# Retention outputs as 64x64 products, issued among the states and the scores of a chunked attention kernel

## The chip, the cores and the metric

The kernel runs on one core of one Trainium2 chip. The metric is device time in microseconds (us) of one launch; the kernel before takes 735.98 us, the median of three runs (735.45 to 736.35). A core has five engines with queues of their own: PE (matmuls, TensorE), DVE (VectorE), ACT (ScalarE), POOL (GpSimd) and SP, which here only issues DMAs; ACT can issue DMAs too.

## The reference, cut to what matters

Three layers follow one another. The change lies in the first.

```
# 1. retention: q, k, v are (8, 8, 576, 64): batch, head, position, head_dim
ret = (q @ k^T / 8) * Dmat          # Dmat = gamma_head ** (i - j) for i >= j, else 0
x   = (ret @ v)  as  (4608, 512)
# 2. x = h * sigmoid(1.702 h) @ w_out,  h = x @ w_in       (512 -> 2048 -> 512)
# 3. soft mixture of experts: logits = x @ phi, softmax over tokens -> 32 slots,
#    two dense layers per expert, softmax over slots -> combine
```

## The kernel before

**Blocks.** The 4608 tokens are 12 blocks of 384. For a block n the big product `hp` (line 316, `main_fc`) takes x(n) times 16 column pieces of w_in, each as 12 matmuls (a split of x and w in a high and a low part), ACT makes `gT` of it (L318), DVE transposes `gT` into a staging buffer (L339, `turn_fc`), and 16 small DMAs on SP's queue carry half a block from there to `nat` (L346, `shuffle`). Logits (`Lg`), the softmax (`lt`, `dp`) and slot sums (`Sg`) of the block before are fitted in between.

**Retention in steps.** x comes from 36 steps, three a block. A step takes one chunk of 64 positions for 2 batches (`NSEQ`) and all 8 heads, that is 4 pairs of heads (`NP`). Every group of 9 steps (`NPB`) goes through one sequence. For each chunk there are three kinds of product, all in fp32 and all 64 columns wide:

- scores `Sp` = K Q (L198), one 64x64 product for each head, two heads of a pair on the two halves of the partitions;
- the running state `St` += K V (L194), 64x64 too;
- the output `Op` (L221, L222): for each head one product over 128 partitions, whose upper and lower halves hold, side by side, scaled state beside raw values (the stationary operand) and raw Q beside decayed scores (the moving one). So state times Q and values times scores are summed in one pass. Its result has 64 rows, so a matmul fills a 128x64 half of the array.

To have these operands stacked, the host lays K, Q, V of the two heads of a pair on opposite halves, a step is loaded by two DMAs of 512 KB (SP lower half, ACT upper half, `load_step`, L165 and L166), and DVE writes the scaled state (L207, L208) and the decayed scores (L212, L213) back into `pack` in four instructions of 64 partitions each. For the first step of a sequence POOL writes zeros in place of the state (L210, L211). POOL scales K (L203). Then DVE scales `Op` to `xs` (L228), ACT casts it to x (L230) and POOL makes the low part (L231).

**Order.** The step of a block's window is called at fc = 4, 9 and 13 of the 16 pieces (`WINDOWS`): first `load_step`, then `step_out` (16 `Op` products), then `products` (16 `St` and 16 `Sp` for the next chunk, interleaved). From block 1 to 10 PE's order is the order of the code (`manual_schedule`); the other engines' order, and PE's in the start (the list `START`, blocks 0 and the first six steps), is set by a scheduler when the program is built. Every engine runs its own list in order. In the start w_in and w_out come in 32 pieces of 512 KB on SP's queue into seven buffers, are converted from 64 bits by ACT, DVE and POOL (L267 to L293) and six of these buffers share their memory with `nat`.

Of the kernel before, what the change touches and what calls it, by code (L numbers as in the profile page):

```python
# [18 lines left out]
B, H, S, D = 8, 8, 576, 64  # L19
# [94 lines left out]
def tile_kernel(ctx, tc, qkv, w_in, w_out, phi, w1, w2, consts, out):  # L114
    nc = tc.nc
    pe, act, dve, pool, sp = nc.tensor, nc.scalar, nc.vector, nc.gpsimd, nc.sync

    pp = ctx.enter_context(tc.tile_pool(name="pp", bufs=1))
    ps = ctx.enter_context(tc.tile_pool(name="ps", bufs=1, space=PSUM))
# [5 lines left out]
    pg = gate_ctx.enter_context(tc.tile_pool(name="pg", bufs=1, reuse_waits="tile"))  # L125
    pb = ctx.enter_context(tc.tile_pool(name="pb", bufs=1, side="right", reuse_waits="tile"))
# [27 lines left out]

    Q1, V0, KT, KN, Q0, V1 = range(6)
    early_raw = pm.tile([128, 6, 1024], F32, tag="nat", name="early_raw")
    packs = [pa.tile([128, 6, NP, NSEQ, C], F32, name=f"pack{i}", bufs=1) for i in range(NPACK)]
    pool.memset(packs[0][0:C, V0], 0.0)  # L160
    pool.memset(packs[0][C:128, V1], 0.0)

    def load_step(g):
        t = packs[g % NPACK].rearrange("p c a j d -> p (c a j d)")
        sp.dma_start(t[0:C, KT * PC:6 * PC], qkv[g, 0:C])  # L165
        act.dma_start(t[C:128, 0:Q0 * PC], qkv[g, C:128])  # L166

    how = {"sub": {}}
    St = {}
    xh, xl = {}, {}  # L170
    halves = (slice(0, C), slice(C, 128))

    def by_head(table, r):
        return table[r].unsqueeze(2).to_broadcast([C, NP, NSEQ, C])

    def by_state(table, r):
        return table.unsqueeze(2).unsqueeze(3).to_broadcast([r, NP, NSEQ, D])

    def products(g):

        n = g + 1
        more = g >= 0 and g % NPB < NPB - 1
        if more:
            if g % NPB == 0:
                St[g // NPB] = ps.tile([128, NP, NSEQ, D], F32, tag="St", name="St")
            s_, t = St[g // NPB], packs[g % NPACK]
        if n < NSTEP:
            u = packs[n % NPACK]
            Sp = ps.tile([128, NP, NSEQ, C], F32, tag="r", name="Sp", bufs=3)
        for p in range(NP):  # L190
            for j in range(NSEQ):
                if more:
                    for h, v in zip(halves, (V1, V0)):
                        pe.matmul(s_[h, p, j, :], t[h, KN, p, j], t[h, v, p, j], start=g % NPB + p + j == 0, stop=True,  # L194
                                  skip_group_check=True)
                if n < NSTEP:
                    for h, o, q in zip(halves, halves[::-1], (Q0, Q1)):
                        pe.matmul(Sp[o, p, j, :], u[h, KT, p, j], u[h, q, p, j], start=True, stop=True)  # L198
        if n == NSTEP:
            return  # L200
        cb = n % NPB
        if cb < NPB - 1:
            pool.tensor_tensor(u[:, KN], u[:, KN], by_state(ksc[:, cb, :], 128), op=ALU.mult)  # L203
        lo, hi = halves
        if more:
            sc = stsc[:, cb, :]
# [8 lines left out]
    def step_out(g):  # L215
        n, i = divmod(g, STEPS)
        t = packs[g % NPACK]
        Op = ps.tile([128, NP, NSEQ, C], F32, tag="r", name="Op", bufs=3)
        for p in range(NP):
            for j in range(NSEQ):  # L220
                pe.matmul(Op[0:C, p, j, :], t[:, V0, p, j], t[:, Q0, p, j], start=True, stop=True)  # L221
                pe.matmul(Op[C:128, p, j, :], t[:, V1, p, j], t[:, Q1, p, j], start=True, stop=True)  # L222
        if n not in xh:
            x = (pg if n % 2 == LAST % 2 else pb).tile([128, 2, NDC, NB], F32R, tag="x", name="x", bufs=1)
            xh[n], xl[n] = x[:, 0], x[:, 1]
        cols_ = slice(i * CP, (i + 1) * CP)
        xs = pa.tile([128, NP, NSEQ, C], F32, tag="xs", name="xs")
        dve.tensor_tensor(xs, Op, osc.unsqueeze(2).to_broadcast([128, NP, NSEQ, C]), op=ALU.mult)  # L228
        flat = xs.rearrange("p a j c -> p a (j c)")
        act.copy(xh[n][:, :, cols_], flat)  # L230
        pool.tensor_tensor(xl[n][:, :, cols_], flat, xh[n][:, :, cols_], op=ALU.subtract)  # L231

    def step_of(g):
        if g + NPACK - 1 < NSTEP:
            load_step(g + NPACK - 1)
        step_out(g)
        products(g)

    wt = {}
    wide = w_in.dtype != F32  # L240
# [34 lines left out]
    def make_wp(i):  # L275
        r0 = 2 * (i % 2)
        for j in range(2):
            fc = 2 * i + j
            wo, free = ring[:, r0 + j, 0], ring[:, r0 + j, 1]
            upper, lower = load_raw((w_out.bitcast(I32) if wide else w_out)[fc * 128:(fc + 1) * 128, :], None)  # L280
            if wide:
                act.activation(upper.bitcast(F32), upper.bitcast(F32), AF.Prelu, scale=2.0 ** -112, alpha=2.0 ** 32)
                dve.tensor_scalar(lower, lower, 29, None, op0=ALU.logical_shift_right)
                dve.scalar_tensor_tensor(wo.bitcast(I32), upper, 3, lower, op0=ALU.logical_shift_left,
                                         op1=ALU.bitwise_or)
            else:
# [13 lines left out]
        dve.transpose(Wp[:, 2 * i:2 * i + 2, :], wps)  # L300
# [227 lines left out]
    n = LAST  # L528
# [18 lines left out]
    n = LAST  # L547
# [203 lines left out]
```

## Time and profile before

| | |
|---|---|
| median of 3 runs | 735.98 us |
| the profiled execution | 738.28 us, span 736.5 us |
| PE busy | 675.6 us (92%) |
| DVE, ACT, POOL busy | 349.5, 230.9, 103.1 us |
| chain that ended last | PE 77%, DMA 9%, DVE 7%, SP's queue 4% |

The profiled execution lies 2.30 us over the median. PE's matmuls overlap, so a long busy time is no sum of their costs; what a matmul costs is read from the distance between the starts of two that follow each other. The span has four parts: the start up to the first `hp`, block 0, an uneven passage into block 1 and ten even blocks of some 47.4 us, then the last block and the third layer.

### The profile page before, as it was taken

What the parts mean: (1) busy time and instruction counts of PE and PEld (TensorE: products, weight loads), DVE (VectorE), ACT (ScalarE), POOL (GpSimd) and SP (SyncE); (2) the same over time, 40 slices, a digit from 0 to 9 for tenths busy, and PEclk for the clock granted to TensorE, in tenths of its full rate; (3) what the DMA queues carried; (4) which work ended last, traced back from release to release, by engine and by line L of the source; (5) the groups of instructions that cost most, each with busy time, mean ns of one, the idle gap of its engine ahead of it and who ended that gap; (6) DMA issues with size and microseconds to landing.
All of it is one profiled execution on the core that took longest, in us unless ns stands there. A gap on an engine that the chain in (4) does not pass through costs nothing.

```text
span 736.5 us, 17854 instructions
## 1 busy us (share of the span) xinstructions
PE 675.6 (92%) x7512; PEld 567.7 (77%) x7512; DVE 349.5 (47%) x964; ACT 230.9 (31%) x431; POOL 103.1 (14%) x93
## 2 busy tenths in 40 slices
PE   2549999699999999999999999999999999978995
PEld 2438879589879899897998988989879788743563
DVE  0786962533554545436454464544554523131233
ACT  0436652222412324123241241332412325231332
POOL 1234320111111111111111021111110000001000
PEclk9769999989999999999999999999999999999999
DMA  9999987638476475574864738637466069899978
GB/s 209 284 294 318 334 237 165 133 75 171 101 152 160 96 156 127 117 165 100 166 145 98 168 80 183 159 82 157 112 144 145 10 204 320 322 409 408 410 285 322
DMA packets 72527, 142.17 MB, mean 193 GB/s; under 512 B 9600, under 2 KB 51840, under 8 KB 67840
## 3 DMA queue, kind: packets, MB, share of 16 engines
q1 hardware_dynamic: 67264, 117.97, 57.1%
q10 hardware_dynamic: 5184, 23.07, 13.3%
q8 instruction: 59, 0.97, 0.6%
q14 instruction: 20, 0.16, 0.1%
HBM read 92.77 MB, written 13.63 MB: 144 GB/s over the span
## 4 chain that ended last, share of the span: by engine, by line
PE 77%; DMA 9%; DVE 7%; SPq 4%; issue 1%; ACT 1%; DVEq 0%; ACTq 0%
PE hp L316 49%; DMA early_raw<-in_moe_w_in_dram 6%; PE Sg L413 5%; PE Op L221 4%; PE Lg L353 4%; PE St L194 3%; PE h_ps L600 3%; PE so_ps L664 3%; SPq L346 2%; DMA pack<-in_qkv_dram 2%; DMA nat<-pre 2%; PE Sp L198 1%; DVE pre L339 1%; SPq L255 1%; PE op L686 1%
## 5 line engine op out<-in xcount | busy, mean ns | idle before, releaser
L316 PE MATMUL hp<-x,w 128*128 128x384 f32 x2304 | 424.1, 341 | 7.6 <-ACT x L230 7.0
L316 PEld LDWEIGHTS hp<-x,w 128*128 128x128 f32 x2304 | 401.3, 189 | 34.9 <-issue 18.6
L318 ACT ACTIVATE gT<-hp 128x384 f32<-128x384 f32 x192 | 94.1, 491 | 317.7 <-PE hp L316 317.6
L339 DVE STREAM_TRANSPOSE ring<-gT 128x128 f32<-128x128 f32 x240 | 55.9, 284 | 120.1 <-ACT gT L318 120.1
L339 DVE STREAM_TRANSPOSE pre<-gT 128x128 f32<-128x128 f32 x288 | 65.3, 281 | 87.8 <-ACT gT L318 77.0
L231 POOL TENSOR_TENSOR x<-xs,x 128x512 fp32r<-128x512 f32 x36 | 46.6, 1296 | 242.7 <-ACT x L230 236.8
L203 POOL TENSOR_TENSOR pack<-pack,cs 128x512 f32<-128x512 f32 x32 | 34.4, 1075 | 179.0 <-DMA pack<-in_qkv_dram 151.7
L198 PE MATMUL Sp<-pack 64*64 64x64 f32 x1152 | 44.2, 228 | 13.5 <-DMA pack<-in_qkv_dram 13.5
L198 PEld LDWEIGHTS Sp<-pack 64*64 64x64 f32 x1152 | 38.6, 140 | 14.5 <-DMA pack<-in_qkv_dram 13.5
L194 PE MATMUL St<-pack 64*64 64x64 f32 x1024 | 40.6, 230 | 9.3 <-DVE pack L208 8.9
L221 PEld LDWEIGHTS Op<-pack 128*64 128x64 f32 x576 | 38.4, 143 | 12.5 <-issue 7.5
L221 PE MATMUL Op<-pack 128*64 128x64 f32 x576 | 44.0, 231 | 4.4 <-DVE pack L212 4.4
L194 PEld LDWEIGHTS St<-pack 64*64 64x64 f32 x1024 | 35.4, 142 | 14.6 <-issue 12.3
L353 PE MATMUL Lg<-gT,Wp 128*32 128x384 f32 x384 | 43.8, 496 | 0.0
L222 PE MATMUL Op<-pack 128*64 128x64 f32 x576 | 43.0, 231 | 0.0
L230 ACT CAST x<-xs 128x512 fp32r<-128x512 f32 x36 | 22.2, 618 | 52.3 <-DVE xs L228 43.8
L222 PEld LDWEIGHTS Op<-pack 128*64 128x64 f32 x576 | 38.0, 143 | 0.4
L413 PE MATMUL Sg<-nat,dn 128*32 128x512 f32 x288 | 35.7, 615 | 0.3 <-DVE dn L397 0.3
L212 DVE TENSOR_TENSOR pack<-Sp,cs 64x512 f32<-64x512 f32 x36 | 25.0, 694 | 11.0 <-PE Sp L198 10.2
L228 DVE TENSOR_TENSOR xs<-Op,cs 128x512 f32<-128x512 f32 x36 | 24.5, 682 | 5.4 <-PE Op L222 5.4
L207 DVE TENSOR_TENSOR pack<-St,cs 64x512 f32<-64x512 f32 x32 | 22.2, 693 | 8.6 <-PE Sp L198 8.4
L413 PEld LDWEIGHTS Sg<-nat,dn 128*32 128x32 f32 x288 | 9.5, 113 | 20.5 <-issue 19.7
(111 smaller groups left out, 485.0 us busy)
## 6 DMA issues: line engine op xcount, KB each, us to landing
wx<-in_moe_w_dram SPq DMA_DIRECT2D x60, 512.0 KB, 10.2
pack<-in_qkv_dram ACTq DMA_DIRECT2D x36, 512.0 KB, 7.5
pack<-in_qkv_dram SPq DMA_DIRECT2D x36, 512.0 KB, 6.9
nat<-pre SPq DMA_DIRECT2D x192, 96.0 KB, 2.3
nat<-ring SPq DMA_DIRECT2D x160, 96.0 KB, 2.2
out_dram<-ob SPq DMA_DIRECT2D x16, 512.0 KB, 3.9
early_raw<-in_moe_w_in_dram SPq DMA_DIRECT2D x14, 512.0 KB, 12.3
early_raw<-in_moe_w_out_dram SPq DMA_DIRECT2D x14, 512.0 KB, 9.3
```

Of the source, the lines that this page charges most:

```text
L194: pe.matmul(s_[h, p, j, :], t[h, KN, p, j], t[h, v, p, j], start=g % NPB + p + j == 0, stop=True, skip_group_check=True)
L198: pe.matmul(Sp[o, p, j, :], u[h, KT, p, j], u[h, q, p, j], start=True, stop=True)
L203: pool.tensor_tensor(u[:, KN], u[:, KN], by_state(ksc[:, cb, :], 128), op=ALU.mult)
L212: dve.tensor_tensor(u[hi, Q0], Sp[hi], by_head(dtab, hi), op=ALU.mult)
L221: pe.matmul(Op[0:C, p, j, :], t[:, V0, p, j], t[:, Q0, p, j], start=True, stop=True)
L222: pe.matmul(Op[C:128, p, j, :], t[:, V1, p, j], t[:, Q1, p, j], start=True, stop=True)
L231: pool.tensor_tensor(xl[n][:, :, cols_], flat, xh[n][:, :, cols_], op=ALU.subtract)
L316: pe.matmul(hp, wt[fc][:, a, dc, :], b[n][:, dc, :], start=(i == 0), stop=(i == 3 * NDC - 1))
L318: act.activation(gT[n, g][:, fl, :], hp, AF.Gelu_apprx_sigmoid)
L339: dve.transpose(dst[:, c], src[:, c])
L353: pe.matmul(Lg[n][32 * fl:32 * fl + 32, :], Wp[:, g * GF + fl, :], gT[n, g][:, fl, :], start=(g == 0), stop=(g == NFC // GF - 1))
L413: pe.matmul(Sg[32 * b:32 * b + 32], dn[n][:, c, :], nv[:, 4 * b:4 * b + 4], start=(c == 0), stop=(c == NT128 - 1))
```

## The change

The output product of a head is taken apart in two 64x64 products that add up in the same place: state times Q (`SS`, `QT`), then values times decayed scores (`VN`, `SC`); at the first chunk of a sequence the first of them is left out. All planes of a head now lie on the same 64 partitions, a step is loaded by one DMA of 1 MB on SP's queue, and `pack` has planes of their own for `SC` and `SS`. DVE writes each by one instruction over 128 partitions, and POOL's zeros are gone. `window` takes the place of `step_out` and `products`: it lists the step's own products (`St`, then `Sp` of the next chunk) and its output products, and issues them in turn, a pair of the one and a pair of the other.

```diff
     def load_step(g):
-        t = packs[g % NPACK].rearrange("p c a j d -> p (c a j d)")
-        sp.dma_start(t[0:C, KT * PC:6 * PC], qkv[g, 0:C])
-        act.dma_start(t[C:128, 0:Q0 * PC], qkv[g, C:128])
+        sp.dma_start(packs[g % NPACK].rearrange("p c a j d -> p (c a j d)")[:, 0:4 * PC], qkv[g])
...
+            for p, j in pairs:
+                if cb:
+                    out_.append((Op, t, SS, QT, p, j, True))
+                out_.append((Op, t, VN, SC, p, j, cb == 0))
...
+            own += [(s_, t, KN, VN, p, j, g % NPB + p + j == 0) for p, j in pairs]
...
+            own += [(Sp, u, KT, QT, p, j, True) for p, j in pairs]
+        for i in range(max(len(own), len(out_))):
+            for what, turn in ((own, 0), (out_, 1)):
+                if i < len(what):
+                    o, w, a, b, p, j, first_ = what[i]
+                    for h, oh in ((lo, (lo, hi)[turn]), (hi, (hi, lo)[turn])):
+                        pe.matmul(o[oh, p, j, :], w[h, a, p, j], w[h, b, p, j], start=first_, stop=True,
                                   skip_group_check=True)
...
+            dve.tensor_tensor(u[:, SC], Sp, across(dtab), op=ALU.mult)
+            if more:
+                dve.tensor_tensor(u[:, SS], s_, by_state(stsc[:, n % NPB, :]), op=ALU.mult)
...
-            dve.tensor_tensor(u[lo, V0], s_[hi], by_state(sc[hi], C), op=ALU.mult)
-            dve.tensor_tensor(u[hi, V1], s_[lo], by_state(sc[lo], C), op=ALU.mult)
-        elif g >= 0:
-            pool.memset(u[lo, V0], 0.0)
-            pool.memset(u[hi, V1], 0.0)
-        dve.tensor_tensor(u[hi, Q0], Sp[hi], by_head(dtab, hi), op=ALU.mult)
-        dve.tensor_tensor(u[lo, Q1], Sp[lo], by_head(dtab, lo), op=ALU.mult)
...
-        for p in range(NP):
-            for j in range(NSEQ):
-                pe.matmul(Op[0:C, p, j, :], t[:, V0, p, j], t[:, Q0, p, j], start=True, stop=True)
-                pe.matmul(Op[C:128, p, j, :], t[:, V1, p, j], t[:, Q1, p, j], start=True, stop=True)
```

PE's order in an even block, at a window (before; the pair of `Op` rows stands eight times, the pair of `St` and `Sp` rows eight times):

```order
L316 MATMUL hp<-x,w 128x384 x84
L221 MATMUL Op<-pack_93 64x64
L222 MATMUL Op<-pack_93 64x64
...
L194 MATMUL St<-pack_93 64x64 x2
L198 MATMUL Sp<-pack_94 64x64 x2
...
L353 MATMUL Lg<-gT,Wp 32x384 x4
L316 MATMUL hp<-x,w 128x384 x12
L366 MATMUL lt<-Lp,sum4r 128x384 x2
```

The same kind of place in the changed kernel (each pair of rows eight times):

```order
L305 MATMUL hp<-x,w 128x384 x24
L202 MATMUL St<-pack_94 64x64 x2
L202 MATMUL Op<-pack_94 64x64 x2
...
L202 MATMUL Sp<-pack_95 64x64 x2
L202 MATMUL Op<-pack_94 64x64 x2
...
L342 MATMUL Lg<-gT,Wp 32x384 x8
```

A window has 64 matmuls in place of 48, and `Op` ends with the window and no longer at its middle.

SP's order at the end of the start, from the last pieces of w_out to block 0's two sets of `nat` transfers (before):

```order
L255 DMA early_raw<-in_moe_w_out_dram 128x1024 x3
L165 DMA pack_94<-in_qkv_dram 64x2048
L455 DMA wx<-wo_dram 128x1024
L346 DMA nat<-pre 32x3x256 x16
L165 DMA pack_95<-in_qkv_dram 64x2048
L455 DMA ring<-in_moe_w_dram 128x1024
L346 DMA nat<-pre 32x3x256 x16
```

And in the changed kernel:

```order
L244 DMA early_raw<-in_moe_w_out_dram 128x1024 x4
L444 DMA wx<-wo_dram 128x1024
L162 DMA pack_94<-in_qkv_dram 128x2048
L335 DMA nat<-pre 32x3x256 x16
L162 DMA pack_95<-in_qkv_dram 128x2048
L335 DMA nat<-pre 32x3x256 x16
L444 DMA ring<-in_moe_w_dram 128x1024
```

The load into `pack_94` stands as a whole ahead of the first `nat` transfers; before, SP issued its lower half one row earlier, and ACT its upper half from its own list. The prefetch into `ring` moves behind the second `nat` transfers.

## Rows read from the trace of the kernel before

**Rows 1.** The page: busy time, then the chain that ended last.

```profile
PE 675.6 (92%) x7512; PEld 567.7 (77%) x7512; DVE 349.5 (47%) x964; ACT 230.9 (31%) x431; POOL 103.1 (14%) x93
...
PE 77%; DMA 9%; DVE 7%; SPq 4%; issue 1%; ACT 1%; DVEq 0%; ACTq 0%
```

**Rows 2.** Busy us of each engine in three stretches, granted clock, DMA share, GB/s.

```profile
13.00:54.08 41.08, 19.92 (x352) 18.01 (x352) 28.65 (x46) 14.07 (x22) 12.26 (x9) 0.75 1.06 282
54.08:107.20 53.12, 51.81 (x635) 43.71 (x635) 41.09 (x84) 31.11 (x56) 18.79 (x14) 0.97 0.98 305
...
146.87:597.30 450.43, 447.67 (x5024) 393.42 (x5024) 225.76 (x679) 127.52 (x233) 62.01 (x55) 0.99 0.58 128
```

**Rows 3.** Timeline of PE in a window: start, length (us), line, tiles.

```profile
263.60 0.27 PE L221 MATMUL Op<-pack 128*64 128x64 f32 x1
...
263.70 0.22 PE L221 MATMUL Op<-pack 128*64 128x64 f32 x1
...
264.52 0.22 PE L221 MATMUL Op<-pack 128*64 128x64 f32 x1
...
264.68 0.27 PE L194 MATMUL St<-pack 64*64 64x64 f32 x2
264.69 0.27 PE L198 MATMUL Sp<-pack 64*64 64x64 f32 x2
...
265.60 0.23 PE L194 MATMUL St<-pack 64*64 64x64 f32 x2
...
265.77 0.85 PE L353 MATMUL Lg<-gT,Wp 128*32 128x384 f32 x8
266.55 15.03 PE L316 MATMUL hp<-x,w 128*128 128x384 f32 x84
```

**Rows 4.** PE's waits from 145 to 600 us, in total, times, longest.

```profile
PE lt L366 <- DVE Lp L360: 2.8, 9, 0.3
```

**Rows 5.** PE's `lt` after the window that starts at 281.51.

```profile
281.51 0.27 PE L221 MATMUL Op<-pack 128*64 128x64 f32 x1
...
287.13 0.62 PE L366 MATMUL lt<-Lp,sum4r 128*128 128x384 f32 x2 [0.31 <-DVE Lp L360]
```

**Rows 6.** DVE's timeline in that window.

```profile
282.20 0.70 DVE L339 STREAM_TRANSPOSE pre<-gT 128x128 f32<-128x128 f32 x3 [1.48 <-ACT gT L318]
...
285.93 0.68 DVE L213 TENSOR_TENSOR pack<-Sp,cs 64x512 f32<-64x512 f32 x1
286.54 0.54 DVE L360 TENSOR_TENSOR Lp<-Lg,Lp 128x384 fp32r<-128x384 f32 x1
```

**Rows 7.** ACT's cast and split there, and POOL's part of x a window earlier.

```profile
283.54 0.62 ACT L230 CAST x<-xs 128x512 fp32r<-128x512 f32 x1 [1.36 <-DVE xs L228]
...
284.61 0.48 ACT L359 CAST Lp<-Lg 128x384 fp32r<-128x384 f32 x1 [0.46 <-PE Lg L353]
...
266.29 1.29 POOL L231 TENSOR_TENSOR x<-xs,x 128x512 fp32r<-128x512 f32 x1 [5.72 <-ACT x L230]
```

**Rows 8.** DVE's groups by line and shape: count, busy us, mean ns.

```profile
L212 DVE TENSOR_TENSOR pack<-Sp,cs 64x512 f32<-64x512 f32 x36 | 25.0, 694 | 11.0 <-PE Sp L198 10.2
...
L228 DVE TENSOR_TENSOR xs<-Op,cs 128x512 f32<-128x512 f32 x36 | 24.5, 682 | 5.4 <-PE Op L222 5.4
```

**Rows 9.** Timeline of PE in the start: its first `hp`.

```profile
54.08 0.69 PE L316 MATMUL hp<-x,w 128*128 128x384 f32 x1 [6.97 <-ACT x L230]
```

**Rows 10.** Chain of waits: SP's first `nat` transfer, start and length.

```profile
106.52 0.66 DVE ring L284
...
107.99 5.82 DMA nat<-pre
```

**Rows 11.** ACT's timeline there.

```profile
107.62 0.98 ACTq L166 DMA_DIRECT2D pack<-in_qkv_dram  x1
```

**Rows 12.** DMA issues: count, KB each, median us to landing.

```profile
pack<-in_qkv_dram SPq DMA_DIRECT2D x36, 512.0 KB, 6.9
nat<-pre SPq DMA_DIRECT2D x192, 96.0 KB, 2.3
```

More of the change, by code (lines that the diff above doesn't have):

```diff
@@ L150, in tile_kernel @@
     phis = pp.tile([128, NDC, NS], F32, name="phis")
-    Q1, V0, KT, KN, Q0, V1 = range(6)
+    KT, KN, QT, VN, SC, SS = range(6)
     early_raw = pm.tile([128, 6, 1024], F32, tag="nat", name="early_raw")
     packs = [pa.tile([128, 6, NP, NSEQ, C], F32, name=f"pack{i}", bufs=1) for i in range(NPACK)]
-    pool.memset(packs[0][0:C, V0], 0.0)
-    pool.memset(packs[0][C:128, V1], 0.0)
     def load_step(g):
-        t = packs[g % NPACK].rearrange("p c a j d -> p (c a j d)")
-        sp.dma_start(t[0:C, KT * PC:6 * PC], qkv[g, 0:C])
-        act.dma_start(t[C:128, 0:Q0 * PC], qkv[g, C:128])
+        sp.dma_start(packs[g % NPACK].rearrange("p c a j d -> p (c a j d)")[:, 0:4 * PC], qkv[g])
     how = {"sub": {}}
@@ L170, in tile_kernel, with across, by_state, window @@
     xh, xl = {}, {}
[L171 to L182, printed above, removed]
+    lo, hi = slice(0, C), slice(C, 128)
+    def across(table):
+        return table.unsqueeze(2).to_broadcast([128, NP, NSEQ, C])
+    def by_state(table):
+        return table.unsqueeze(2).unsqueeze(3).to_broadcast([128, NP, NSEQ, D])
+    def window(g):
+        n, cb = g + 1, g % NPB
+        more = g >= 0 and cb < NPB - 1
+        pairs = [(p, j) for p in range(NP) for j in range(NSEQ)]
+        own, out_ = [], []
+        if g >= 0:
+            t = packs[g % NPACK]
+            Op = ps.tile([128, NP, NSEQ, C], F32, tag="r", name="Op", bufs=3)
+            for p, j in pairs:
+                if cb:
+                    out_.append((Op, t, SS, QT, p, j, True))
+                out_.append((Op, t, VN, SC, p, j, cb == 0))
         if more:
-            if g % NPB == 0:
+            if cb == 0:
                 St[g // NPB] = ps.tile([128, NP, NSEQ, D], F32, tag="St", name="St")
-            s_, t = St[g // NPB], packs[g % NPACK]
+            s_ = St[g // NPB]
+            own += [(s_, t, KN, VN, p, j, g % NPB + p + j == 0) for p, j in pairs]
         if n < NSTEP:
@@ L189, in products @@
             Sp = ps.tile([128, NP, NSEQ, C], F32, tag="r", name="Sp", bufs=3)
-        for p in range(NP):
-            for j in range(NSEQ):
-                if more:
-                    for h, v in zip(halves, (V1, V0)):
-                        pe.matmul(s_[h, p, j, :], t[h, KN, p, j], t[h, v, p, j], start=g % NPB + p + j == 0, stop=True,
-                                  skip_group_check=True)
-                if n < NSTEP:
-                    for h, o, q in zip(halves, halves[::-1], (Q0, Q1)):
-                        pe.matmul(Sp[o, p, j, :], u[h, KT, p, j], u[h, q, p, j], start=True, stop=True)
@@ L199, in products @@
-        if n == NSTEP:
-            return
[L201 to L206, printed above, removed]
-            dve.tensor_tensor(u[lo, V0], s_[hi], by_state(sc[hi], C), op=ALU.mult)
-            dve.tensor_tensor(u[hi, V1], s_[lo], by_state(sc[lo], C), op=ALU.mult)
-        elif g >= 0:
-            pool.memset(u[lo, V0], 0.0)
-            pool.memset(u[hi, V1], 0.0)
@@ L212, in products @@
-        dve.tensor_tensor(u[hi, Q0], Sp[hi], by_head(dtab, hi), op=ALU.mult)
-        dve.tensor_tensor(u[lo, Q1], Sp[lo], by_head(dtab, lo), op=ALU.mult)
[L215 to L220, printed above, removed]
-                pe.matmul(Op[0:C, p, j, :], t[:, V0, p, j], t[:, Q0, p, j], start=True, stop=True)
-                pe.matmul(Op[C:128, p, j, :], t[:, V1, p, j], t[:, Q1, p, j], start=True, stop=True)
-        if n not in xh:
-            x = (pg if n % 2 == LAST % 2 else pb).tile([128, 2, NDC, NB], F32R, tag="x", name="x", bufs=1)
-            xh[n], xl[n] = x[:, 0], x[:, 1]
+            own += [(Sp, u, KT, QT, p, j, True) for p, j in pairs]
@@ new lines, in window @@
+        for i in range(max(len(own), len(out_))):
[4 more added lines that the diff above has]
+                        pe.matmul(o[oh, p, j, :], w[h, a, p, j], w[h, b, p, j], start=first_, stop=True,
+                                  skip_group_check=True)
+        if n < NSTEP:
+            if n % NPB < NPB - 1:
+                pool.tensor_tensor(u[:, KN], u[:, KN], by_state(ksc[:, n % NPB, :]), op=ALU.mult)
+            dve.tensor_tensor(u[:, SC], Sp, across(dtab), op=ALU.mult)
+            if more:
+                dve.tensor_tensor(u[:, SS], s_, by_state(stsc[:, n % NPB, :]), op=ALU.mult)
@@ L226, in step_out @@
+        if g < 0:
+            return
+        b_, i = divmod(g, STEPS)
+        if b_ not in xh:
+            x = (pg if b_ % 2 == LAST % 2 else pb).tile([128, 2, NDC, NB], F32R, tag="x", name="x", bufs=1)
+            xh[b_], xl[b_] = x[:, 0], x[:, 1]
         cols_ = slice(i * CP, (i + 1) * CP)
         xs = pa.tile([128, NP, NSEQ, C], F32, tag="xs", name="xs")
-        dve.tensor_tensor(xs, Op, osc.unsqueeze(2).to_broadcast([128, NP, NSEQ, C]), op=ALU.mult)
+        dve.tensor_tensor(xs, Op, across(osc), op=ALU.mult)
@@ L229, in step_out @@
         flat = xs.rearrange("p a j c -> p a (j c)")
-        act.copy(xh[n][:, :, cols_], flat)
-        pool.tensor_tensor(xl[n][:, :, cols_], flat, xh[n][:, :, cols_], op=ALU.subtract)
+        act.copy(xh[b_][:, :, cols_], flat)
+        pool.tensor_tensor(xl[b_][:, :, cols_], flat, xh[b_][:, :, cols_], op=ALU.subtract)
     def step_of(g):
@@ L235, in step_of @@
             load_step(g + NPACK - 1)
-        step_out(g)
-        products(g)
+        window(g)
     wt = {}
@@ L464, in tile_kernel @@
     outs = [lambda i=i: make_wp(i) for i in range(NFC // 2)]
-    items = [lambda: products(-1)] + [lambda g=g: step_of(g) for g in range(2 * STEPS)]
+    items = [lambda: window(-1)] + [lambda g=g: step_of(g) for g in range(2 * STEPS)]
     def step(x):
@@ L736 @@
     q, k, v = inputs["q"], inputs["k"], inputs["v"]
-    lower = np.concatenate([turned(k, 0), rows(k, 1), turned(q, 0), rows(v, 1)], axis=2)
-    upper = np.concatenate([turned(q, 1), rows(v, 0), turned(k, 1), rows(k, 0)], axis=2)
-    host = {"qkv": np.ascontiguousarray(np.concatenate([lower, upper], axis=1)), **host}
+    side = lambda h: np.concatenate([turned(k, h), rows(k, h), turned(q, h), rows(v, h)], axis=2)
+    host = {"qkv": np.ascontiguousarray(np.concatenate([side(1), side(0)], axis=1)), **host}
     host["consts"] = _CONSTS
```

## Prediction

> **What bounds the kernel now.** I read the page first: PE is busy 92% of the span and the chain that ended last runs 77% through it [rows 1]. That is a mean over parts with different limits, so the table by stretches comes next. From 146.87 to 597.30 us PE works 447.67 of 450.43 us at full clock, with the DMA share at 0.58: ten blocks in which only PE's own issue counts [rows 2]. From 54.08 to 107.20 PE is busy 51.81 of 53.12 us, but the DMA share is 0.98 too, and before 54.08 PE is idle more than half of the time while the DMA engines are full [rows 2]. So a change pays in the even blocks by what PE issues, and at the start by what it does to the DMA stream and to the order of DVE's list.
>
> In an even block I then read one window matmul by matmul. An fp32 product appears as two records. In the output half two 128x64 products side by side start every 0.058 us: 263.70 to 264.52 in 14 steps, each step one record of either column half. In the other half four 64x64 quarters start in the same distance, two records of `St` and two of `Sp` [rows 3]. So a quarter array costs 0.058 / 4 us a record whichever shape carries it, and both halves already fill the array. What is not filled is the joints: the first pair takes 0.10 us (263.60 to 263.70), and 0.16 us lie between the last `Op` and the first `St` (264.52 to 264.68), 0.17 between the last `St` and `Lg` (265.60 to 265.77) [rows 3]. The window is 2.17 us long (263.60 to 265.77).
>
> **PE in the windows.** An ordinary window loses 16 full output products and gets 32 quarter ones: 32 products x 2 records / 4 in a step = 16 steps of 0.058, as before. So it has 32 steps without the joint in the middle: 0.10 + 30 x 0.058 + 0.17 = 2.01 us in place of 2.17, 0.16 saved. The first chunk of a sequence has 8 output pairs less but then runs the 8 `Sp` pairs alone, with half the array idle: 8 x 2 filled steps and 8 x 2 half-filled ones, again 32. The last chunk has no `St`, so 16 steps are filled and the other 8 output pairs run alone: 32 steps, where before `Sp` alone took as long as `St` with `Sp`. All these save 0.16. Only the very last window, outputs alone, goes from 16 steps to 32: 0.93 more. In the ten blocks 29 x 0.16 - 0.93 = 3.7 us saved. That the array takes a quarter `Op` in the place of a quarter `Sp` at the same pace is what rows 3 show for `St` beside `Sp`; the one new thing is that two products in a row add up in one place. Bounds: nothing saved but the 0.93 lost (+0.9), up to 0.2 a window (-5).
>
> **DVE.** Four instructions of 64 partitions at about 0.69 us become two of 128 partitions. A 128-partition read of a matmul result with a table beside it is `xs`, 0.682 us, no dearer than 64 partitions at 0.694 [rows 8]. So each step takes 1.4 us off DVE, some 48 us in all, of an engine that is busy 47% [rows 1]; it counts only where PE waits for DVE. In the even blocks that is one place: `lt` waits 0.31 us for `Lp`, 9 times, 2.8 us in all [rows 4, 5]. `Lp` is late because DVE does four evictions first (until 286.61) [rows 6]. Now, from the window's start at 281.51: DVE is free of its transposes at 1.39 [rows 6]; the state's eviction runs to 2.1, the scores' to 2.8, `xs`, which now stands third since `Op` ends with the window, to 3.5; ACT casts until 4.1 and splits until 4.6, both 0.62 and 0.48 long [rows 7]; DVE's part of `Lp` (0.54, rows 6) ends at 5.2. `lt` starts at about 5.26 where it started at 5.62 [rows 5]. Of the 0.36 the shorter window holds 0.16, so 0.2 x 9 = 1.8 us more. Bounds: 0, if the later `xs` eats it, and 2.8.
>
> **x comes later.** In the window ahead of a new block `Op` ended at the middle; now it ends at 2.0, and `xs` at 3.5. ACT's cast takes it to 4.1 and POOL's part (1.29, rows 7) to 5.4. The next block's first `hp` comes after `Lg` (0.78) and two pieces of 12 matmuls at 15.03 / 84 = 0.179 [rows 3]: 2.01 + 0.78 + 4.29 = 7.1. The slack is 1.7 us, so this costs nothing; if DVE or ACT were that much later it would cost ten times the excess.
>
> **Loads.** The same bytes come, in 36 transfers of 1 MB on one queue. Between two windows of the even blocks lie at least four pieces, 48 x 0.179 = 8.6 us of `hp`, and half a load lands 6.9 us after its issue [rows 12]; the two halves already shared the engines, so I take the whole to land about as late as the later half. Cost nothing; 1 us a window if a load were late. POOL's zeros were off the path.
>
> **The start.** Up to the first `hp` at 54.08 [rows 9] DMA is the bound at 282 GB/s [rows 2]. Counted in DVE's and SP's lists, the third `xs` stands behind 8 pieces of w_in, 4 of w_out, four lower and five upper halves (10.5 MB) before, and behind 9, 5 and four whole loads (11 MB) now. That is 0.5 MB or 1.8 us later, if the queue were strictly in order; against it the DVE has 4 us less to do in those steps, and the first piece of w_in no longer shares its way with all three upper halves. I take 0 (-4 to +5). Between 54.08 and 107.20, where PE is the bound, three windows save 0.16 each: 0.5 us. Then SP has to carry block 0 to `nat`, which it may do after the last conversion of w_out at 106.52 to 107.18; the first transfer takes 5.82 us [rows 10] where the median is 2.3 [rows 12]. Right before it ACT issued half a load at 107.62 [rows 11]. In the changed list this load stands on SP ahead of the transfers and can go as soon as the window that used its buffer is over. So up to 3.5 us may go; I take 2, since writes of w_out compete there as well.
>
> **Sum.** 738.28 - 3.7 - 1.8 - 0.5 - 2 = 730.3 for an execution like the profiled one. That one lies 2.30 us over the median of the runs, so the forecast is 735.98 - 8.0 = **728.0 us**.
>
> **Rivals.**
>
> *Only PE's joints pay.* `Lp` stays as late, since `xs` and the cast now come in front of it, and the first `nat` transfer still takes 5.8 us because of w_out's writes: 735.98 - 3.7 = 732.3. For it: ACT's list has the cast ahead of the split, and both need the end of the window. Against: two evictions less.
>
> *The start gets ahead.* With 1.4 us of DVE work less in each of six steps and conversions waiting for DVE, the first `hp` comes 4 us earlier and PE follows, as it has 1.3 us of idle time in 53: about 724. Against: the DMA share of 1.06 before 54.08 [rows 2] leaves nothing to win if the same bytes must come.
>
> *No joint is saved.* Two output products in a row into one place do not follow at 0.058, or quarter `Op` beside `St` costs an extra 0.01 a step: 29 x 0.16 is lost again, only the 0.93 and DVE's gains remain: about 735.5, no change.
>
> *Slower: the loads in one queue hold up the weights.* The upper halves of the fourth to the eighth load (5 x 0.5 MB, 1.75 us each at 305 GB/s, rows 2) stood in a queue beside SP's; now they stand in front of pieces of w_in and w_out. If each delays the chain of weights by its full time, and the third `xs` by 1.8 on top, that is +10.5 against the 8.0 of gains: 738.5. It is slower than before from 8 us on. For it: the chain through the start runs over w_in's transfers and SP's queue. Against: the engines were full anyway, and the bytes ahead of a piece are nearly the same.
>
> *One bank, two row halves.* In the changed window both row halves of the array write the same result bank for `Op`; before one 128-row product did. If they could not, the output half would double: 29 x 0.93 = 27 us, 755. `St` alone does this already, both halves of it in one step of 0.058 [rows 3]. [...]
>
> **How the numbers follow.** Forecast 0.40 (its own range 724.5 to 731.5), PE's joints alone 0.20, the start ahead 0.12, no joint saved 0.12, loads in one queue 0.13, one bank 0.03. About 0.2%, 1.5 us, is what a measurement of this kernel can tell from no change. Faster 0.40 + 0.20 + 0.12 = 0.72, same 0.12, slower 0.16. The range of 8 in 10 takes the first four cases and the near half of the slow one: 722 to 738.
>
> **What would show it.** In the even blocks a window's distance from first product to `Lg` should be 2.0 us, a block some 0.5 us shorter, and `lt`'s wait gone or 0.1. At a block's start no wait for ACT's or POOL's x. In the last window 0.93 more. In the start: the first `hp` at 50 to 57 us, the first `nat` transfer near 3 us. The prediction is wrong if steps of a window lie further apart than 0.058, if `hp` waits for x at block starts, or if the first `hp` comes after 60.

## The result and the profile after

The changed kernel takes 715.28 us, the median of four runs (714.22 to 718.83), against 735.72 for the kernel before on the same chip: a ratio of 0.9737 (95% interval 0.9695 to 0.9779). That is 20.4 us less where 8.0 were forecast, below the lower end of the range. The profiled execution took 718.83 us, its span is 717.0 against 736.5.

The page after: the first lines of busy time and of the chain, which answer to [rows 1], and the DMA queues (packets, MB, share of 16 engines).

```profile
PE 665.1 (93%) x8536; PEld 562.9 (79%) x8536; DVE 303.0 (42%) x896; ACT 229.9 (32%) x431; POOL 98.1 (14%) x85
...
q1 hardware_dynamic: 69568, 136.84, 60.4%
q10 hardware_dynamic: 2304, 4.20, 1.5%
...
PE 84%; DVE 6%; SPq 4%; DMA 3%; issue 1%; ACT 1%; DVEq 0%; ACTq 0%
```

The same two queues on the page before:

```profile
q1 hardware_dynamic: 67264, 117.97, 57.1%
q10 hardware_dynamic: 5184, 23.07, 13.3%
```

The reader is to see that the same 141.04 MB took 70.4% of the DMA engines' time before and 61.9% after: the loads that ACT's queue carried before are in SP's queue now, at a better pace.

**Where the time went.** The first `Sg` product of a block is a good mark for comparing. PE's timeline before has it here (start, length; the first, the tenth and the last of them):

```profile
157.67 1.90 PE L413 MATMUL Sg<-nat,dn 128*32 128x512 f32 x16
...
584.22 2.33 PE L413 MATMUL Sg<-nat,dn 128*32 128x512 f32 x20
...
658.27 2.79 PE L413 MATMUL Sg<-nat,dn 128*32 128x512 f32 x12 [0.35 <-DVE dn L397]
```

And after, with the first `hp`, which answers to [rows 9]:

```profile
43.46 0.69 PE L305 MATMUL hp<-x,w 128*128 128x384 f32 x1 [4.63 <-ACT x L220]
...
145.06 1.47 PE L402 MATMUL Sg<-nat,dn 128*32 128x512 f32 x12
...
563.67 1.90 PE L402 MATMUL Sg<-nat,dn 128*32 128x512 f32 x16
...
639.03 1.94 PE L402 MATMUL Sg<-nat,dn 128*32 128x512 f32 x8 [0.35 <-DVE dn L386]
```

| part | before | after | difference |
|---|---|---|---|
| start to the first `Sg` | 157.67 | 145.06 | -12.6 |
| nine block lengths up to the tenth | 426.55 | 418.61 | -7.9 |
| to the last `Sg` | 74.05 | 75.36 | +1.3 |
| to the end of the span | 78.2 | 78.0 | -0.2 |

The sum is the 19.4 us between the spans (19.5 by their rounded lengths). The start gave 12.6 where 2.5 were forecast; all that follows gave 6.8 where 5.5 were forecast.

The start by stretches, which answers to [rows 2] (busy us of PE, PEld, DVE, ACT, POOL, then the granted clock, DMA share and GB/s):

```profile
13.00:43.46 30.46, 11.51 (x289) 10.76 (x289) 26.40 (x40) 15.59 (x25) 11.60 (x9) 0.64 1.05 384
43.46:92.15 48.69, 47.14 (x617) 40.05 (x618) 36.02 (x74) 28.67 (x51) 16.69 (x13) 0.94 0.86 301
145.06:563.70 418.64, 418.64 (x5549) 371.84 (x5545) 178.82 (x601) 121.76 (x225) 58.58 (x50) 1.00 0.50 135
```

Up to the first `hp` the DMA engines are as full as before (1.05 against 1.06), and they carry 384 GB/s in place of 282. From 145.06 to 563.70 PE is never idle.

One window in PE's timeline after, in place of [rows 3] (the middle is left out), and `lt`, which no longer waits [rows 4, 5]:

```profile
220.34 0.27 PE L202 MATMUL St<-pack 64*64 64x64 f32 x2
220.35 0.27 PE L202 MATMUL Op<-pack 64*64 64x64 f32 x2
...
221.26 0.23 PE L202 MATMUL St<-pack 64*64 64x64 f32 x2
221.27 0.22 PE L202 MATMUL Op<-pack 64*64 64x64 f32 x2
221.32 0.22 PE L202 MATMUL Sp<-pack 64*64 64x64 f32 x2
221.33 0.23 PE L202 MATMUL Op<-pack 64*64 64x64 f32 x2
...
222.21 0.23 PE L202 MATMUL Op<-pack 64*64 64x64 f32 x2
222.36 0.85 PE L342 MATMUL Lg<-gT,Wp 128*32 128x384 f32 x8
223.14 2.38 PE L305 MATMUL hp<-x,w 128*128 128x384 f32 x12
225.43 0.61 PE L355 MATMUL lt<-Lp,sum4r 128*128 128x384 f32 x2
```

From the second on, the steps lie 0.058 us apart to the end, no joint stands between `St` and `Sp` (221.26 to 221.32), and the window is 2.02 us long (220.34 to 222.36).

**The packets.** The trace also holds the time of each DMA packet. Medians worked out from them, in ns:

```
                                       before   after
K, Q, V loads, packets of 8 KB           612     309     (ACT's half before: 606)
weights, packets of 4 KB                 161     161
packets of 2 KB                           84      84
packets of 1 KB, w_in                     49      46
packets of 1 KB, nat                      76      76
```

(The first 8192 packets of 1 KB are w_in's; the last of them starts before the first `nat` transfer.) Of these only the loads' packets changed by more than 3 ns: 13.4 bytes per ns before, 26.5 now, which is the pace the weights' 4 KB packets always had (25.4). A load of 1 MB is 128 of them, so it took 128 x 303 / 16 = 2.4 us of all 16 engines more than it does now. Five to six loads lie before the first `hp`: 12 to 14.5 us by this estimate, 10.6 measured (54.08 to 43.46).

### The profile page after: what moved, and what is told of

Same layout as the page of the kernel before. It is cut to its first block, busy times and chain, and to the rows that moved or that the text cites. A ratio compares the mean times of both kernels' runs of the same rounds, so it can differ in the third digit from the quotient of the medians.

```text
span 717.0 us, 19711 instructions
## 1 busy us (share of the span) xinstructions
PE 665.1 (93%) x8536; PEld 562.9 (79%) x8536; DVE 303.0 (42%) x896; ACT 229.9 (32%) x431; POOL 98.1 (14%) x85
## 4 chain that ended last, share of the span: by engine, by line
PE 84%; DVE 6%; SPq 4%; DMA 3%; issue 1%; ACT 1%; DVEq 0%; ACTq 0%
PE hp L305 54%; PE Lg L342 5%; PE Sg L402 5%; PE St L202 3%; PE Sp L202 3%; SPq L335 3%; PE h_ps L589 2%; PE so_ps L653 2%; PE Op L202 2%; DMA early_raw<-in_moe_w_in_dram 2%; PE op L675 1%; DVE pre L328 1%; DVE early_raw L258 1%; PE lt L355 1%; PE tpw L279 1%
## 5 line engine op out<-in xcount | busy, mean ns | idle before, releaser
L202 PE MATMUL Op<-pack 64*64 64x64 f32 x2176 | 74.9, 225 | 6.7 <-DVE pack L207 6.7
L202 PEld LDWEIGHTS Op<-pack 64*64 64x64 f32 x2176 | 69.6, 140 | 7.7 <-DVE pack L207 7.0
L202 PE MATMUL Sp<-pack 64*64 64x64 f32 x1152 | 42.4, 226 | 7.0 <-DMA pack<-in_qkv_dram 7.0
L207 DVE TENSOR_TENSOR pack<-Sp,cs 128x512 f32<-128x512 f32 x36 | 24.7, 685 | 12.0 <-PE Sp L202 7.4
L408 DVE SCALAR_TENSOR_TENSOR acc<-acc,corr,Sg 128x512 f32<-128x512 f32 x11 | 8.2, 748 | 37.0 <-PE Sg L402 37.0
L209 DVE TENSOR_TENSOR pack<-St,cs 128x512 f32<-128x512 f32 x32 | 21.0, 656 | 0.4 <-PE St L202 0.4
L653 PE MATMUL so_ps<-wx,hT 128*32 128x128 f32 x512 | 18.6, 275 | 1.2 <-issue 1.2
```

The lines of the kernel that those rows point to most:

```text
L202: pe.matmul(o[oh, p, j, :], w[h, a, p, j], w[h, b, p, j], start=first_, stop=True, skip_group_check=True)
L207: dve.tensor_tensor(u[:, SC], Sp, across(dtab), op=ALU.mult)
L653: pe.matmul(SR[q][32 * j:32 * j + 32, :], hT[e // 4][:, e % 4, f, :], wx[2, q, e][:, f, :], start=(e == 0 and f < 4), stop=(e == NE - 1 an ...
```

## Experiments

The theory after the result: a load onto 64 of the 128 partitions carries its packets at half the pace (612 against 309 ns for 8 KB), and where the DMA stream is the bound, that is paid in full; one load over all partitions is what gave the start. Rivals: that the loads stand in one queue in place of two; that they are fewer and larger; that DVE has two evictions in place of four. All kernels were timed beside the kernel before on the same chip; ratios are to it. One thing varies along with most edits: the scheduler lays the start out anew when the loads or DVE's instructions change, so few of these kernels share one order of DVE's list there.

**Halves on two queues, and on one.** The changed kernel, its load cut by partitions; in the second kernel SP issues both.

```diff
-        sp.dma_start(packs[g % NPACK].rearrange("p c a j d -> p (c a j d)")[:, 0:4 * PC], qkv[g])
+        t = packs[g % NPACK].rearrange("p c a j d -> p (c a j d)")
+        sp.dma_start(t[0:C, 0:4 * PC], qkv[g, 0:C])
+        act.dma_start(t[C:128, 0:4 * PC], qkv[g, C:128])
```

> The changed kernel with each step's load in two again, as before: lower 64 partitions on SP, upper 64 on ACT. All else as changed. Theory 'shape' (a load onto 64 partitions carries its 8 KB packets at half the pace: 612 ns a packet in the trace of before, 309 after): packets go back to about 610 ns, the first hp comes after 50 us again (43.5 changed, 54.1 before) and the time goes up by 8 to 14 us, to 723 to 729. Rival 'queues' (two queues in flight slow each other): the same here. Rival 'DVE' (the start got shorter because DVE has 1.4 us less to do a step): stays within 2 us of 715.

> The changed kernel with each step's load as two transfers of 64 partitions, both on SP's queue. Theory 'shape': packets of about 610 ns if the halves lie one behind the other in the queue, 723 to 729 us. Rival 'queues': packets near 310 ns and 715 us, as only one queue carries loads. Rival 'DVE': 715.

On two queues 738.91 us (ratio 1.0049, 1.0022 to 1.0077), on one 734.84 (0.9972, 0.9954 to 0.9990). Packets take 602 to 622 ns again, the first `hp` stands at 57.37 and 53.31, and from 10 to 50 us the stream runs at 288 and 291 GB/s. The even blocks keep their new length of 46.5 us. So the start's gain hangs on the width of the load. One queue is 4 us faster than two, the other direction than the slower rival had it; the order of the start differs too, so this is not shown for the queue alone. Both kernels end above the 723 to 729 expected: with half loads they lose in the start (first `Sg` at 166.4 and 163.8, 8.7 and 6.2 us later than before) all or nearly all that they gain in the blocks. Why their start is longer than before stays open.

**Planes on two queues, and on one.** The load cut by columns instead: K's two planes, then Q's and V's, each over 128 partitions; in the second kernel SP issues both.

```diff
-        sp.dma_start(packs[g % NPACK].rearrange("p c a j d -> p (c a j d)")[:, 0:4 * PC], qkv[g])
+        t = packs[g % NPACK].rearrange("p c a j d -> p (c a j d)")
+        sp.dma_start(t[:, 0:2 * PC], qkv[g][:, 0:2 * PC])
+        act.dma_start(t[:, 2 * PC:4 * PC], qkv[g][:, 2 * PC:4 * PC])
```

> The changed kernel with each step's load in two transfers of 128 partitions and 4 KB a partition, K planes on SP, Q and V planes on ACT. Theory 'shape': packets of 4 KB near 160 ns as for the other 4 KB transfers, first hp at 42 to 46 us, 713 to 718 us. Rival 'queues': packets at twice that and 723 to 729 us. Rival 'DVE': 715.

> The changed kernel with each step's load as two transfers of 128 partitions and 4 KB a partition, both on SP's queue. Theory 'shape': as changed in the start (first hp 42 to 46 us) and in the even blocks (46.5 us), since POOL's K scaling no longer waits for ACT's list ahead of x: 713 to 718 us. If two transfers a step cost something by themselves (semaphores, order), it shows here: above 720.

The start is that of the changed kernel: 4 KB packets at 159 ns, 385 GB/s, first `hp` at 44.38 and 45.07, first `Sg` at 146.5 and 145.9. So the width gives the start, however the bytes are cut and queued. This holds whatever the order: the seven kernels here with loads over 128 partitions and no edit of the start's other transfers have their first `Sg` at 142.4 to 147.6 us, the three with loads over 64 at 157.7 to 166.4. The times do not follow it, against what was expected: 739.39 (1.0042, 1.0023 to 1.0060) and 733.42 (0.9973, 0.9953 to 0.9993). Most of the loss, 18.1 and 14.0 us, lies in three of the even blocks, which take 50.5 to 53.3 us. PE's wait in one of them, and POOL's timeline before it (planes on one queue):

```profile
356.98 1.33 PE L307 MATMUL hp<-x,w 128*128 128x384 f32 x3 [2.48 <-POOL x L223]
```

```profile
354.67 1.04 POOL L208 TENSOR_TENSOR pack<-pack,cs 128x512 f32<-128x512 f32 x1 [13.98 <-DMA pack<-in_qkv_dram]
355.67 1.26 POOL L223 TENSOR_TENSOR x<-xs,x 128x512 fp32r<-128x512 f32 x1
```

With two transfers a step the scheduler put the scaling of the next chunk's K ahead of x's low part on POOL, K waits for its load, and x waits behind K. That was tried next.

**x first.** The planes on one queue, with POOL's order from block 1 on as the code has it and the scaling of K behind x.

```diff
-    with tc.manual_schedule(engines={mybir.EngineType.PE}):
+    with tc.manual_schedule(engines={mybir.EngineType.PE, mybir.EngineType.Pool}):
...
-            if n % NPB < NPB - 1:
-                pool.tensor_tensor(u[:, KN], u[:, KN], by_state(ksc[:, n % NPB, :]), op=ALU.mult)
...
         pool.tensor_tensor(xl[b_][:, :, cols_], flat, xh[b_][:, :, cols_], op=ALU.subtract)
+        if n < NSTEP and n % NPB < NPB - 1:
+            pool.tensor_tensor(u[:, KN], u[:, KN], by_state(ksc[:, n % NPB, :]), op=ALU.mult)
```

> planes_one_queue (a load as two transfers of 128 partitions, K planes and then Q and V planes, both on SP), but POOL's order from block 1 on is the order of the code, with the scaling of K behind x's low part. In planes_one_queue POOL scaled the next chunk's K, which waits for its load, ahead of x in three blocks, and hp waited 2.19 to 2.82 us for x there. If POOL's order was what cost it 18 us against the changed kernel, the three long blocks go back to 46.5 and the time is 717 to 722 (the last part of the 18 us lies behind the ten blocks). If two transfers for a step cost by themselves, it stays at 730 to 734.

720.01 us (0.9787, 0.9756 to 0.9819), and the three blocks take 46.4 to 46.8. So POOL's order was 13 us of the loss; some 4 us against the changed kernel stay, of which 2 to 3 lie ahead of the first `Sg` (147.4, against 145.1 and 144.1 in two profiles of the changed kernel).

**The kernel before with one padded load.** The old products and evictions, but all six planes of `pack` come as one load of 1.5 MB over 128 partitions, with zeros in the two planes of each half that DVE writes later.

```diff
-        sp.dma_start(t[0:C, KT * PC:6 * PC], qkv[g, 0:C])
-        act.dma_start(t[C:128, 0:Q0 * PC], qkv[g, C:128])
+        sp.dma_start(t, qkv[g])
...
-        elif g >= 0:
-            pool.memset(u[lo, V0], 0.0)
-            pool.memset(u[hi, V1], 0.0)
...
+    lower = np.concatenate([none, lower], axis=2)
+    upper = np.concatenate([upper, none], axis=2)
```

> The kernel before with its products, evictions and layout, but each step's load as one transfer over all 128 partitions and six planes on SP's queue: 1.5 MB, of which the planes that DVE overwrites are zeros (so POOL's zeros are left out too). Theory 'shape': 12 KB packets in about 460 ns, 128 x 0.46 / 16 = 3.7 us of all engines a load in place of 2 x 64 x 0.61 / 16 = 4.9, though half as many bytes again come; the first hp 5 to 7 us earlier than 54.1 and the time 727 to 732. If the load's shape did not matter, half as many bytes more would make the start longer: 738 to 746.

727.85 us (0.9896, 0.9863 to 0.9929): with half as many bytes again the kernel is 8 us faster. Packets of 12 KB take 460 ns, 26.7 bytes per ns. The first `hp` comes at 34.71, 19 us earlier than before, but the first `Sg` only 10 (147.56): then PE waits in block 0, mostly for DVE's `ring` (five waits, 8.4 us). The even blocks are as before (47.42, 47.24). No other run comes as near to the load's part of the change by itself, though POOL's zeros are gone here too and the order differs. The order also fits a first `hp` that came so much earlier than the 5 to 7 us expected: 11 of DVE's instructions on weights (`early_raw`) stand ahead of it, where there were 19 before and 21 in the changed kernel. The first `Sg`, behind all of them, is the better measure.

**Four evictions.** The changed kernel with DVE's scores and states written in four instructions of 64 partitions.

```diff
-            dve.tensor_tensor(u[:, SC], Sp, across(dtab), op=ALU.mult)
+            for h in (lo, hi):
+                dve.tensor_tensor(u[h, SC], Sp[h], dtab[h].unsqueeze(2).to_broadcast([C, NP, NSEQ, C]), op=ALU.mult)
...
-                dve.tensor_tensor(u[:, SS], s_, by_state(stsc[:, n % NPB, :]), op=ALU.mult)
+                sc = stsc[:, n % NPB, :]
+                for h in (lo, hi):
+                    dve.tensor_tensor(u[h, SS], s_[h],
+                                      sc[h].unsqueeze(2).unsqueeze(3).to_broadcast([C, NP, NSEQ, D]), op=ALU.mult)
```

> The changed kernel with DVE's scores and state written by four instructions of 64 partitions again, as before (1.4 us more of DVE a step). Theory 'shape': the start moves by less than 3 us; in the even blocks the wait of lt for Lp comes back, 0.3 to 0.8 us a block, x still in time: 717 to 724 us. Rival 'DVE': the first hp goes back towards 54 us and the time to 725 to 730.

717.07 us (0.9734, 0.9706 to 0.9762), first `hp` at 43.0, first `Sg` at 142.4. So DVE's merge gives the start nothing that shows. It saves 4.2 us of evictions ahead of the first `hp` (5.4 against 9.6), but the 21 instructions on `early_raw` (weights) there take 15.9 us in the changed kernel's order and 12.4 in this one. In the blocks it gives what it was to give: from the first `hp` behind `Lg` to `lt` PE needs 2.66 us before, 2.50 here and 2.29 in the changed kernel.

**Not in turn.** The window's own products first, all output products behind them.

```diff
-        for i in range(max(len(own), len(out_))):
-            for what, turn in ((own, 0), (out_, 1)):
+        for what, turn in ((own, 0), (out_, 1)):
+            for i in range(len(what)):
```

> The changed kernel with the same products in another order: the step's own products (state, then scores) first, then its output products, none in turn with the other. A step of the window then fills half the array. If four quarters at once are what makes quarter outputs free, a window takes 64 steps of 0.058 us in place of 32, 3.9 in place of 2.0 us, 30 x 1.86 = 56 us more, about 770 us. If the array did not care which quarters follow each other, the time stays at 715.

756.91 us (1.0286, 1.0244 to 1.0329). A window in PE's timeline:

```profile
258.05 1.15 PE L202 MATMUL St<-pack 64*64 64x64 f32 x32
259.03 0.93 PE L202 MATMUL Sp<-pack 64*64 64x64 f32 x26
...
259.91 1.91 PE L202 MATMUL Op<-pack 64*64 64x64 f32 x59
261.75 0.53 PE L342 MATMUL Lg<-gT,Wp 128*32 128x384 f32 x4
```

It is 3.70 us long in place of 2.02: 64 half-filled steps at 0.058 in place of 32 filled ones. Nine block lengths are 457.1 in place of 418.6, which is nearly the whole difference. The 770 expected was too much: a window is 3.7 and not 3.9 us, six of these 27, at the first and last chunk of a sequence, take only 2.77, and those of the start cost next to nothing (first `Sg` at 145.9), where PE has waits to take them in. So the turn-taking carries the even blocks: with it the 64x64 products win 7.9 us there, without it they lose 30.6 against the kernel before.

**Weights in rows.** The changed kernel with w_in laid out by the host in rows of 4 KB in place of 1 KB, to see whether the stream still bounds the start.

```diff
-        n = 256 if wide else 128
-        src = (w_in.bitcast(I32) if wide else w_in)[:, fc * n:(fc + 1) * n].rearrange("(c p) f -> p c f", p=128)
+        src = (w_in.bitcast(I32) if wide else w_in)[fc].rearrange("p (c f) -> p c f", c=NDC)
...
+    host["moe_w_in"] = np.ascontiguousarray(
+        host["moe_w_in"].reshape(NDC, 128, NFC, 128).transpose(2, 1, 0, 3).reshape(NFC, 128, NDC * 128))
```

> The changed kernel with w_in laid out by piece on the host, so that a piece comes as 4 KB rows and not as 1 KB rows: 128 packets of 160 ns in place of 512 of 73 ns, 1.3 us of all engines a piece in place of 2.3. If the DMA stream is still what bounds the start, the 9 pieces ahead of the third xs give up to 9 us: first hp at 35 to 40 us, 706 to 711 us. If DVE is the bound there by now (9.7 of 10 us busy from 20 to 40), less than 3 us: 712 to 716.

715.46 us (0.9741, 0.9699 to 0.9782), no different from the changed kernel, with the first `hp` at 42.9 and the first `Sg` at 141.7. The edit had less to give than was reckoned: the 73 ns of the expectation is the median of all 1 KB packets, of which four in five are `nat`'s. w_in's own take 46 (mean 50), so a piece cost 512 x 50 / 16 = 1.6 us of all engines, not 2.3, and costs 128 x 175 / 16 = 1.4 now (175 is the mean of the 4 KB packets there): some 2 us for nine pieces, not 9. From 10 to 50 us the stream went from 387 to 406 GB/s. The start by stretches, columns as above:

```profile
20.00:30.00 10.00, 3.40 (x82) 3.05 (x75) 9.69 (x13) 4.69 (x8) 4.33 (x3) 0.50 1.02 411
30.00:40.00 10.00, 4.87 (x128) 4.57 (x126) 9.31 (x16) 5.83 (x11) 3.56 (x3) 0.67 1.02 406
```

DVE is busy 9.69 and 9.31 of 10 us here, and 9.69 in both stretches of the changed kernel. There the chain that leads to the first `hp` runs mostly through DVE's list from 19.8 to 42.8 us, where before it ran through DMA transfers: that stretch has a new bound, and the faster stream brought the first `hp` forward by 0.3 to 0.6 us only. Not all of this busy time need be work. DVE's timeline in the changed kernel has one line of the program twice:

```profile
21.04 0.43 DVE L257 TENSOR_SCALAR early_raw<-early_raw 128x512 int32<-128x512 int32 x1
...
22.18 1.53 DVE L257 TENSOR_SCALAR early_raw<-early_raw 128x512 int32<-128x512 int32 x1
```

The second runs beside POOL's L262 (21.93 to 23.42) and ends 0.3 us behind it. From 20 to 42 us there are six such instructions, 5.5 us longer in all than their like; each ends 0.3 to 0.6 us behind one of POOL's. That POOL held them up fits these rows, but no run tried it.

**The second `nat` set on two queues.** What PE still waits for in the changed kernel's passage into block 1 is one `lt`. DVE's transposes ahead of it stand idle until the second `nat` set, which SP issues one by one, is through (PE's, DVE's and SP's timelines; the wait of DVE's first row is put down to the `ring` transfer that SP issues right behind the set):

```profile
131.15 1.01 PE L355 MATMUL lt<-Lp,sum4r 128*128 128x384 f32 x2 [5.86 <-DVE Lp L349]
...
125.84 3.01 DVE L328 STREAM_TRANSPOSE pre<-gT 128x128 f32<-128x128 f32 x15 [13.87 <-DMA ring<-in_moe_w_dram]
...
110.74 11.68 SPq L335 DMA_DIRECT2D nat<-pre  x16
```

```diff
-                sp.dma_start(nat[n][32 * b:32 * b + 32, :, a, hf * HF:(hf + 1) * HF, :],
+                q = act if n == 0 and hf == 1 and b % 2 else sp
+                q.dma_start(nat[n][32 * b:32 * b + 32, :, a, hf * HF:(hf + 1) * HF, :],
...
```

> The changed kernel, but of the 16 nat transfers of block 0's second half 8 are issued by ACT instead of SP. In the changed kernel these 16 take SP 11.7 us (110.74 to 122.4), DVE's transposes of block 1 wait for their buffer until 125.84, and PE's lt waits 5.86 us for DVE at 131.15. If that last wait of the start is the issue pace of SP, the set is out in about 6 us, lt's wait falls to under 1 us, the first Sg comes at about 140 and the kernel takes 709 to 711. If ACT's issues (some 0.7 us each) come in front of its gT evictions, hp waits for them instead and the time stays at 714 to 717. If the transfers themselves set the pace and not their issue, nothing changes: 715.

713.38 us (0.9696, 0.9674 to 0.9718), first `Sg` at 140.5. The rows that answer:

```profile
110.65 6.97 ACTq L336 DMA_DIRECT2D nat<-pre  x8
...
121.46 3.02 DVE L328 STREAM_TRANSPOSE pre<-gT 128x128 f32<-128x128 f32 x15 [9.62 <-DMA nat<-pre]
...
118.22 4.45 PE L305 MATMUL hp<-x,w 128*128 128x384 f32 x24 [2.33 <-ACT gT L307]
```

The first two theories both had a part: the transposes come 4.4 us earlier (2.2 against the second profile of the changed kernel, below), now released by `nat`, and `lt` no longer waits, and ACT's issues of 0.87 us each hold up gT, which costs `hp` 2.33.

**Both edits of the start.** The last two together, beside the changed kernel once more.

> The changed kernel once more, as the measure for the next one on the same chip: 715 (714 to 719), first hp near 43.5 us, first Sg near 145, lt waiting 5.9 us for DVE near 131.

> w_in laid in rows of 4 KB by the host (first Sg at 141.7 by itself) and half of block 0's second nat set issued by ACT (first Sg at 140.5 and 713.4 by itself). If the two gains lie in different places of the start, the weights' stream and the passage into block 1, they add up: first Sg near 137, and 709 to 711. If earlier weights only make the passage wait longer, the first Sg stays near 140 and the time at 713 to 714.

The changed kernel again took 716.09 us (714.82 to 717.48; ratio 0.9734, 0.9700 to 0.9769), with `lt` waiting 3.62 us in this profile; both edits 712.50 (711.7 to 714.9; 0.9692, 0.9660 to 0.9724), first `Sg` at 139.7. That is 3.6 us under the changed kernel on the same chip and the lowest median of all, but hardly under the second `nat` set alone: the gains do not add up.

## Why the prediction was wrong

**The step that failed** is in the part on loads and the start: "the two halves already shared the engines, so I take the whole to land about as late as the later half. Cost nothing", and from it "I take 0 (-4 to +5)" for the first `hp`. It moved by -10.6, and the first `Sg` by -12.6. I counted bytes and their order and took 282 GB/s at a share of 1.06 [rows 2] for a full stream. A share of busy time says that packets are under way, not at what pace: 1.06 went with 282 GB/s before and 1.05 with 384 after. The two halves shared the engines, but each packet held its engine twice as long (612 against 309 ns).

That was to be read before: the loads had 612 ns for 8 KB where weights had 161 for 4 KB, and on the page ACT's queue took 13.3% of the engines' time for 23.07 MB where SP's took 57.1% for 117.97, many of them in 1 KB packets. A sum from it (five to six loads x 2.4 us) would have given 12 to 14.5 us in the start.

What halves the pace, no run shows. The runs show that it goes with the 64 partitions, 612 against 309 ns a packet, and that it is no better with the halves on two queues (602 and 622) than on one (611).

**The slower rival** (the loads in one queue hold up the weights) had the sign wrong for the same reason. Halves on one queue were 4 us faster than on two (734.84 against 738.91).

**The start gets ahead** was the rival nearest to what happened, at 724, by the wrong mechanism: it had DVE's saved work for a cause, which four evictions speak against (first `hp` at 43.0 without it), and I set against it that a DMA share of 1.06 left nothing to win. Now it is mostly DVE that bounds that stretch (busy 9.69 of 10 us from 20 to 30 and from 30 to 40).

**PE's joints** were right: 2.17 to 2.02 a window, three windows of a block 6.52 to 6.08, so 0.44 where 0.48 was forecast; the last window costs 0.91 more (`Sg` to `Sg` 38.03 to 38.94, forecast 0.93). Behind it 0.4 more is lost (36.01 to 36.42), where the granted clock is 0.96 against 0.99. Neither "no joint is saved" nor "one bank, two row halves" came: two output products in a row into one place follow at 0.058, from both row halves. That the halves write one bank was my reading of the kernel; the rows show one tile, `Op`, and no banks.

**DVE and `lt`**: the mechanism was right and the term too small, 0.37 a block, in every third 0.44 (2.66 to 2.29 or 2.22), where 0.2 was taken. I reckoned `lt` at 5.26 us behind the window's start, still held by `Lp`; it comes at 5.09 (220.34 to 225.43) and waits for nothing, since each link of the chain through ACT was a little sooner than reckoned (the split at 3.97, not 4.1). With the joints this makes some 0.84 of the 0.88 a block; the rest stays open.

**x comes later** cost nothing, as forecast: PE's list of waits from 145 to 600 us is empty. How thin that cover is, planes on two queues show: x 2 to 4 us later is 4 to 7 us a block.

**The first `nat` transfer** was reckoned at 2 us less. The transfers do land as fast as forecast (2.2 us where the first took 5.82), but from the set's first issue to the transposes that wait for it 13.7 us pass (92.15 to 105.83) in place of 14.4 (107.20 to 121.59), of which SP's sixteen issues take 11.6 (12.5 before). So this gave 0.7, and the second set's wait stayed, 5.86 us at `lt` where `dp` had waited 6.10 before. The passage as a whole gave 2.0 (first `hp` to first `Sg`: 103.6 to 101.6), and that this is near the 2.5 taken for it is luck: 4.4 were won ahead of the first `nat` issue (53.12 to 48.69), for which 0.5 was forecast, and 2.4 lost behind it (50.47 to 52.91). Where the 4.4 come from stays open.

## What to carry to other kernels

Read GB/s and time per packet beside the DMA share: a stream can be full of slow packets (a share of 1.06 at 282 GB/s here, of 1.05 at 384). A tile stacked from two halves was worth loading over all 128 partitions at once here, even with half as many bytes again (727.85 us against 735.98); what that brought was paid out only where the stream was the bound, and only until the next engine was (19 us at the first `hp` of that run, 10 at its first `Sg`). Take a packet's time from the transfers that are meant: a median over all packets of a size mixed w_in's 46 ns with `nat`'s 76. After a change of the loads, look at the order of every engine that a scheduler lays out, since one operation that waits for a load, put in front of one that PE waits for, cost 13 us here (733.42 to 720.01).

## What was not expected of the hardware

A pause of PE cost more than its length here. In planes on one queue PE waits 2.48 us for x at a granted clock of 0.98 and then runs at 0.50 for some 3.3 us (columns as above):

```profile
354.50:356.98 2.48, 0.00 (x0) 0.00 (x0) 0.70 (x3) 0.35 (x1) 2.26 (x2) 0.98 0.16 61
356.98:358.00 1.02, 1.02 (x3) 1.02 (x4) 0.00 (x0) 0.00 (x0) 0.00 (x0) 0.50 0.71 169
358.00:360.00 2.00, 2.00 (x7) 2.00 (x7) 0.00 (x0) 0.00 (x0) 0.00 (x0) 0.50 0.63 150
360.00:362.00 2.00, 2.00 (x12) 2.00 (x12) 0.70 (x3) 0.49 (x1) 0.00 (x0) 0.93 0.63 148
362.00:367.00 5.00, 5.00 (x31) 5.00 (x30) 1.40 (x6) 1.04 (x3) 0.00 (x0) 1.00 0.59 140
```

Half the clock for 3.3 us is 1.6 lost, by estimate: the block is 4.1 us longer (50.75 against 46.68) for a wait of 2.48. In the three long blocks of this run the waits are 7.5 us and the blocks 14.0 us longer. And a quarter of the array in fp32 took the same step of 0.058 us here whichever product filled it, `St`, `Sp` or `Op`, also where two products in a row add up in one place and both row halves write one tile, `Op`.
